# A fused gated long convolution and MLP on one core: the first loads in another order and on two queues, shared copies in tiles of their own, and the last output tile in halves

## The chip, the cores and the metric

The kernel runs on one core of one Trainium2 chip, as one launch. TensorE (PE) multiplies, and PEld is its weight load; VectorE (DVE), ScalarE (ACT) and GpSimd (POOL) do the other arithmetic; SyncE (SP) only issues transfers, and ACT issues some too. The two queues of transfers are q1 (issued by SP) and q10 (issued by ACT) in the profile. The metric is device time in microseconds (us), the median over runs.

## The reference

All inputs are bfloat16, with S = 2048 tokens and D = 512 channels; `F` stands for 1376 hidden columns.

```python
def _A_ref(q, k, v, shift_k, ssm_k, ssm_D):
    k_shift = sum over t in 0..3 of k_pad[:, t:t + S, :] * shift_k[:, 3 - t]
    kv = k_shift * v
    y = irfft(rfft(kv padded to 2S) * rfft(ssm_k padded to 2S))[:S]   # along the tokens
    y = y + kv * ssm_D
    return q * y

x = A_q
h = x + _A_ref(_layernorm(x), A_k, A_v, A_shift_k, A_ssm_k, A_ssm_D)
h2 = h + relu(_layernorm(h) @ w1) @ w2
```

So there is a short convolution over four tokens (the taps), a product with v, a convolution over all tokens with one filter for each channel (ssm_k), a gate with the normalised input, a residual, and an MLP with a residual.

## The kernel before

The order of the work is written out by hand: each engine takes its instructions in the order of the program, and waits by semaphores. PSUM tiles come from a ring of four tiles of two banks each (`bank2`); a fifth tile waits until the users of the first are done with it.

**Opening (L122 to L239).** SP issues, in this order, shift_k (`wsh`, L123), ssm_k (`sk`, 2 MB, L124), and then k and v in four pieces of 512 tokens each, transposed on the way (L134, L136, L137): k0, v0, k1, v1 and so on, about 0.5 MB each. ACT issues two loads of ssm_D (`draw`, 1 KB each, L128). PE runs 22 matmuls on zeros meanwhile (`fill`, L158). POOL makes index tables and two identity matrices (`identw` in float32, then `ident` in bfloat16, L176), `r2` (iota at L180), then `dmask` from ssm_D with 16 small copies (L236), and multiplies `r2` (L238). DVE turns shift_k into float32 (`wf`, L191), works out angles (`_turns`, L44 and L46), then the tables `f1hi` and `f1lo` for stage 1 (L210 to L215), and `tsn` (L222, and `wrap13` at L220). ACT computes the sines (L147) and 16 diagonal matrices `wdiag` (L204), which are the identity scaled by one tap of one group of 128 channels.

**Rows of ssm_k (`to_rows`, L271).** PE transposes ssm_k 128x128 at a time, eight to a PSUM tile, in four steps h = 0 to 3. ACT copies the tiles of h = 0 and 2, DVE that of h = 1, and the tile of h = 3 is copied half by ACT and half by DVE. The same function later turns the product kv around (L388).

**Stage 1 (`stage1`, L286) and taps (`taps`, L329).** The loop at L343 runs gb = 0 to 6. A step of stage 1 is 32 small matmuls into two PSUM tiles; DVE adds `dmask` to half of each (L306), ACT casts the other halves (L309). A tap unit `taps(c, h)` takes a piece c of the tokens and two groups of channels: eight matmuls of `wdiag` with shifted k into one PSUM tile (L333), and one product with v on DVE (L337). Behind step gb stands tap unit (gb // 2, gb % 2), and the last two, (3, 0) and (3, 1), stand ahead of step 6. ACT has sines between its casts (L226, then L262). Behind the loop follow v's rows, step 7, and eight steps for kv, whose tiles ACT and DVE copy into BX (L267, L269).

**Middle and inverse (L402 to L541).** Products in the transformed domain, then `inv1(b, eng)` for b = 0 to 15: twelve matmuls into one PSUM tile, which ACT or DVE copies out as two pieces. At b = 15 both do: ACT groups 0 and 1, DVE groups 2 and 3 of the same tile. The next PE work is `inv2(0)` (tile `pz`, L613).

**MLP (`mlp1`, `mlp2`).** `mlp2(sc)` (L631) runs four tiles of 128 tokens: eleven matmuls of 512 columns (L638), one DVE operation that scales and adds (L641), and a store of 128 KB issued by ACT (L644). The last tile is t = 15.

## Time and profile before

| | us |
|---|---|
| median of 3 runs (215.8 to 216.24) | 216.12 |
| the profiled execution's own time | 215.98 |
| its span, first to last instruction | 214.2 |
| PE busy | 202.7 (95%) |
| DVE busy | 140.8 (66%) |
| ACT busy | 114.9 (54%) |
| POOL busy | 61.6 (29%) |

The span is 1.8 us shorter than the execution's time, which holds what lies ahead of the first and behind the last instruction. The granted PE clock is full in all slices. Busy shares are means over stages. What an edit is worth is read from the stage in which it stands: from what PE waits for there, and from what stands in each queue behind an operation that moves.

### The profile page before, as it was taken

How to read it: one execution, taken by the hardware profiler on the slowest of the kernel's cores; microseconds unless marked ns; L12 is line 12 of the kernel's file. 1: busy time of each engine (PE TensorE's matmuls, PEld its weight loads, DVE VectorE, ACT ScalarE, POOL GpSimd, SP SyncE). 2: the span in 40 equal slices, each digit the busy share in tenths (PEclk: the TensorE clock that was granted, in tenths of full speed). 3: DMA queues.
4: the chain of work that ended last, by engine and by line, in shares of the span. 5: the costliest groups of instructions: out<-in, count | busy, mean ns of one | idle time of the engine just before them, and what ended most of it. 6: DMA issues, size and time to landing. Idle time of an engine off the chain costs nothing. (4 is left out here: it accounts for less than half of the span.)

```text
span 214.2 us, 4311 instructions
## 1 busy us (share of the span) xinstructions
PE 202.7 (95%) x1736; PEld 138.1 (64%) x1736; DVE 140.8 (66%) x243; ACT 114.9 (54%) x185; POOL 61.6 (29%) x116
## 2 busy tenths in 40 slices
PE   7879999999999999999997999999999999999990
PEld 2465555888888888799996964448444844444440
DVE  5968988598778878889753397499249825261121
ACT  6687776687776777645495029601970065027200
POOL 7954704994555500032003012511201120002000
PEclk9999999999999999999999999999999999999999
DMA  5999940001600000036504996977955532410011
GB/s 152 342 226 177 221 77 2 3 5 25 245 0 0 3 0 3 0 98 101 98 3 127 273 216 117 191 129 129 108 58 100 120 74 29 98 55 17 0 51 47
DMA packets 47686, 19.91 MB, mean 93 GB/s; under 512 B 42706, under 2 KB 46132, under 8 KB 47668
## 3 DMA queue, kind: packets, MB, share of 16 engines
q1 hardware_dynamic: 44144, 16.15, 39.2%
q10 hardware_dynamic: 3524, 3.51, 5.7%
q8 instruction: 13, 0.21, 0.4%
q14 instruction: 5, 0.04, 0.1%
HBM read 7.02 MB, written 2.10 MB: 43 GB/s over the span
## 5 line engine op out<-in xcount | busy, mean ns | idle before, releaser
L627 ACT ACTIVATE M<-ps1m 128x512 bf16<-128x512 f32 (+1 forms) x44 | 25.0, 602 | 49.9 <-PE ps1m L625 39.4
L638 PE MATMUL ps2m<-M 128*128 128x512 bf16 (+1 forms) x176 | 38.7, 379 | 0.0
L638 PEld LDWEIGHTS <-M 128*128 128x128 bf16 (+1 forms) x176 | 17.1, 98 | 20.9 <-ACT M L627 0.4
L625 PEld LDWEIGHTS <-w 128*128 128x128 bf16 (+1 forms) x176 | 17.4, 100 | 20.4 <-issue 0.8
L380 POOL TENSOR_TENSOR smc<-st 64x256 fp32r<-64x256 f32 x32 | 22.7, 729 | 11.1 <-PE us L427 10.2
L641 DVE SCALAR_TENSOR_TENSOR M<-ps2m,rstd,M 128x512 bf16<-128x512 f32 x12 | 8.9, 746 | 22.0 <-PE ps2m L638 13.1
L531 PE MATMUL psi<-inv,BK 128*128 128x256 f32 x128 | 23.1, 283 | 0.1
L481 POOL TENSOR_SCALAR rstd<-mv 128x4 f32<-128x4 f32 x8 | 2.2, 275 | 68.9 <-DVE mv L479 68.9
L434 DVE TENSOR_TENSOR BK<-u,ktu 128x512 fp32r<-128x512 f32 x32 | 20.4, 680 | 0.0
L531 PEld LDWEIGHTS psi<-inv,BK 128*128 128x128 f32 x128 | 20.1, 195 | 0.3 <-DVE BK L434 0.3
L625 PE MATMUL ps1m<-xT,w 128*128 128x512 bf16 (+1 forms) x88 | 19.6, 379 | 0.2 <-ACT M L627 0.2
L625 PE MATMUL ps1m<-M,w 128*128 128x512 bf16 (+1 forms) x88 | 19.3, 379 | 0.0
L531 PE MATMUL psi<-inv,BX 128*128 128x256 f32 x64 | 18.2, 286 | 0.0
L407 ACT COPY ktu<-u 128x512 f32<-128x512 f32 x32 | 17.2, 589 | 1.5
L434 DVE TENSOR_TENSOR BX<-us,kts 128x512 fp32r<-128x512 f32 x16 | 11.1, 691 | 8.4 <-PE u L417 6.7
L417 PE MATMUL u<-BK,st 64*128 64x256 f32 x128 | 14.6, 308 | 0.0
L407 ACT COPY kts<-us 128x512 f32<-128x512 f32 x16 | 9.4, 587 | 9.5 <-PE us L427 9.5
L417 PE MATMUL u<-BX,st 64*128 64x256 f32 x128 | 13.0, 284 | 0.0
L309 ACT CAST BK<-ps 128x512 fp32r<-128x512 f32 x16 | 9.4, 585 | 6.5 <-PE ps L294 3.9
L531 PEld LDWEIGHTS psi<-inv,BX 128*128 128x128 f32 x64 | 12.4, 195 | 0.3 <-DVE BK L434 0.2
L477 DVE BATCH_NORM_STATS2 st<-M 128x6 f32<-128x512 bf16 x20 | 12.3, 678 | 0.0
L599 DVE TENSOR_TENSOR qT<-pz,qT 128x2048 bf16<-128x2048 f32 x2 | 4.6, 2291 | 11.3 <-DMA qT<-M 7.3
(123 smaller groups left out, 399.0 us busy)
## 6 DMA issues: line engine op xcount, KB each, us to landing
E<-in_A_ssm_k_dram SPq DMA_DIRECT2D x1, 2048.0 KB
out_dram<-M ACTq DMA_DIRECT2D x16, 128.0 KB
w<-in_B_w_dram SPq DMA_DIRECT2D x1, 1376.0 KB
M<-in_B_w_dram ACTq DMA_DIRECT2D x1, 1280.0 KB
M<-in_A_q_dram SPq DMA_DIRECT2D x8, 128.0 KB
xh<-in_A_q_dram SPq DMA_DIRECT2D x4, 128.0 KB
xr<-in_A_q_dram SPq DMA_DIRECT2D x4, 128.0 KB
M<-in_B_w_dram ACTq DMA_DIRECT2D x1, 96.0 KB
```

Of the source, the lines that this page charges most:

```text
L309: nc.scalar.copy(out=o[1 - rp][:, 1], in_=pv[1 - rp][:, 1])
L380: nc.gpsimd.tensor_tensor(out=smc[pq, c % 4, i, :, 64 * dp:64 * dp + 64], in0=st[pq, ks, 64:128].bitcast(F32), in1=st[pq, ks, 0:64].bitcas ...
L407: nc.scalar.copy(out=kt[:], in_=ps)
L417: nc.tensor.matmul(out=ps[:, dp, 256 * x:256 * x + 256], lhsT=t[pq], rhs=cols((BK, BX)[x], pq, k1, i), start=(i == 0), stop=(i == 1), tile ...
L434: nc.vector.tensor_tensor(out=o, in0=ps[:, :, 256:512].rearrange("p b (g x) -> p b g x", x=8), in1=kt[:].rearrange("p b (g x) -> p b g x", ...
L477: nc.vector.bn_stats(out=st[:, i, :], in_=src[:, i, :])
L531: nc.tensor.matmul(out=o, lhsT=src[:, g // 2, :, g % 2::2].rearrange("p c r -> p (c r)"), rhs=rhs, start=(part == 0), stop=(part == 2), sk ...
L599: nc.vector.tensor_tensor(out=flat(qT[q]), in0=pzs[q][:].rearrange("p i r a n -> p (i r a n)"), in1=flat(qT[q]), op=ALU.mult)
L625: nc.tensor.matmul(out=ps1[:fsz, :].rearrange("p (i t) -> p i t", i=4), lhsT=w1[:, c, fc * P:fc * P + fsz], rhs=hT[sc][:, :, c, :], start= ...
L627: nc.scalar.activation(out=h1T[:fsz, fc, :], in_=ps1[:fsz, :], func=ACT.Relu)
L638: nc.tensor.matmul(out=ps2[:], lhsT=h1T[:ksz, fc, i * P:(i + 1) * P], rhs=w2[:ksz, fc, :], start=(fc == 0), stop=(fc == NFC - 1))
L641: nc.vector.scalar_tensor_tensor(out=o[:], in0=ps2[:], scalar=rstd2[:, t, :], in1=xh[sc][:, i, :], op0=ALU.mult, op1=ALU.add)
```

## The change

- **Loads.** The loads of shift_k and ssm_k move from SP's queue to ACT's, ahead of the two loads of ssm_D. SP's queue then begins with k0. The zeroing of two tiles on DVE comes ahead in the text.
- **Identities.** POOL makes `ident` before `identw`.
- **wdiag.** Of the 16 scalings, the eight for the first two groups of channels go to DVE, the other eight stay on ACT, ahead of the first two sines. `_turns` for t3 and the work on `tsn` change places with the tables f1.
- **Taps.** `taps(0, 0)` and `taps(0, 1)` move ahead of the rows of ssm_k, behind 14 of the matmuls on zeros; six more of these follow them. In the loop, the tap units behind the steps are now (1, 0), (1, 1), (2, 0), none, (2, 1), none.
- **Tiles of their own.** In `to_rows` at h = 3 and in `inv1` at b = 15, ACT's and DVE's parts each get a PSUM tile.
- **Last tile.** For t = 15, `mlp2` runs two halves of 256 columns, each with eleven matmuls, one DVE operation and one store of 64 KB.

In the built program ACT's order at the start is: load of shift_k, load of ssm_k, two loads of ssm_D (the second waits for shift_k's semaphore), a table load, eight scalings, a table load, sines.

```diff
-    nc.sync.dma_start(out=wsh[:], in_=A_shift_k.rearrange("(r p) j -> p r j", p=P))
-    nc.sync.dma_start(out=sk, in_=A_ssm_k.rearrange("(c p) t -> p c t", p=P))
+    nc.scalar.dma_start(out=wsh[:], in_=A_shift_k.rearrange("(r p) j -> p r j", p=P))
+    nc.scalar.dma_start(out=sk, in_=A_ssm_k.rearrange("(c p) t -> p c t", p=P))
     draw = small([DC * P], BF16)
     for dp in range(2):
...
-    fill(bank2("psz")[:, 0, :], 22)
+    psz = bank2("psz")[:, 0, :]
+    fill(psz, 14)
...
-    for t in (identw, ident):
+    for t in (ident, identw):
...
+            if rg < 2:
+                nc.vector.tensor_scalar(out=wdiag[:, rg, j, :], in0=ident[:], scalar1=wf[:, rg, j:j + 1], scalar2=None, op0=ALU.mult)
+            else:
+                nc.scalar.mul(out=wdiag[:, rg, j, :], in_=ident[:], mul=wf[:, rg, j:j + 1])
...
+    taps(0, 0)
+    taps(0, 1)
+    fill(psz, 6)
...
-        pst = bank2("pst").rearrange("p b (i c) -> p (b i) c", i=4)
...
-        for i in range(8):
-            nc.tensor.transpose(out=pst[:, i, :], in_=srcw[:, :, 8 * h + i], identity=identw[:])
...
+        for eng, i0, n in {1: (("D", 0, 8),), 3: (("A", 0, 4), ("D", 4, 4))}.get(h, (("A", 0, 8),)):
+            pst = bank2("pst").rearrange("p b (i c) -> p (b i) c", i=4)[:, 0:n]
+            for i in range(n):
+                nc.tensor.transpose(out=pst[:, i, :], in_=srcw[:, :, 8 * h + i0 + i], identity=identw[:])
...
+    behind = {0: (1, 0), 1: (1, 1), 2: (2, 0), 4: (2, 1)}
...
-        if gb < 6:
-            taps(gb // 2, gb % 2)
+        if gb in behind:
+            taps(*behind[gb])
...
-        ps = bank2("psi").rearrange("p b (i d a n) -> p (b i) d a n", i=2, d=2, a=2)
...
         for e, i0, n in ((eng, 0, 4),) if len(eng) == 1 else ((eng[0], 0, 2), (eng[1], 2, 2)):
+            ps = bank2("psi").rearrange("p b (i d a n) -> p (b i) d a n", i=2, d=2, a=2)[:, 0:n]
...
+            w = D // 2 if t == NT - 1 else D
+            for d0 in range(0, D, w):
+                ps2 = psm.tile([P, D], F32, tag="ps", name="ps2m")[:, 0:w]
```

More of the change, by code (lines that the diff above doesn't have):

```diff
@@ L122 @@
     wsh = consts.tile([P, DC, KS], BF16, name="wsh")
-    nc.sync.dma_start(out=wsh[:], in_=A_shift_k.rearrange("(r p) j -> p r j", p=P))
-    nc.sync.dma_start(out=sk, in_=A_ssm_k.rearrange("(c p) t -> p c t", p=P))
+    zero = consts.tile([P, 512], BF16, name="zero")
+    nc.vector.memset(zero[:], 0.0)
+    nc.vector.memset(kT[0][:, :, 0:16], 0.0)
+    nc.scalar.dma_start(out=wsh[:], in_=A_shift_k.rearrange("(r p) j -> p r j", p=P))
+    nc.scalar.dma_start(out=sk, in_=A_ssm_k.rearrange("(c p) t -> p c t", p=P))
     draw = small([DC * P], BF16)
@@ L128 @@
         nc.scalar.dma_start(out=draw[64 * dp:64 * dp + 1, :], in_=src)
-    zero = consts.tile([P, 512], BF16, name="zero")
-    nc.vector.memset(zero[:], 0.0)
-    nc.vector.memset(kT[0][:, :, 0:16], 0.0)
     for c in range(4):
@@ L194 @@
     _turns(nc, t1[:, 32:64], r1[:], n1c[:], 128, False)
+    f1f = small([64], F32)
+    f1d = small([64], F32)
+    for rg in range(DC):
+        for j in range(KS):
+            if rg < 2:
+                nc.vector.tensor_scalar(out=wdiag[:, rg, j, :], in0=ident[:], scalar1=wf[:, rg, j:j + 1], scalar2=None, op0=ALU.mult)
+            else:
+                nc.scalar.mul(out=wdiag[:, rg, j, :], in_=ident[:], mul=wf[:, rg, j:j + 1])
+    _sin(f1f[:, 0:32], t1[:, 0:32], 128)
+    _sin(f1f[:, 32:64], t1[:, 32:64], 128, neg=True)
     t3 = small([2, 64], I32)
@@ L197 @@
     _turns(nc, t3[:, 1, :], r3[:], n2c[:], 64, False)
-    f1f = small([64], F32)
-    f1d = small([64], F32)
-    _sin(f1f[:, 0:32], t1[:, 0:32], 128)
-    _sin(f1f[:, 32:64], t1[:, 32:64], 128, neg=True)
-    for rg in range(DC):
-        for j in range(KS):
-            nc.scalar.mul(out=wdiag[:, rg, j, :], in_=ident[:], mul=wf[:, rg, j:j + 1])
     dsc = small([2, 64], F32)
@@ L207, with wrap13 @@
     _sin(dsc[:], t3[:], 64)
+    st = stp.tile([P, 32, 192], F32R, name="st")
+    def wrap13(t):
+        nc.vector.tensor_scalar(out=t, in0=t, scalar1=19, scalar2=19, op0=ALU.logical_shift_left, op1=ALU.arith_shift_right)
+    nc.vector.tensor_single_scalar(out=tsn, in_=r2, scalar=n2c[:], op=ALU.mult)
+    wrap13(tsn)
     f1h = small([64], BF16)
@@ L215, with taps @@
             nc.vector.tensor_copy(out=f[rows, :, rg % 2], in_=src[rows, :].rearrange("p (h w v) -> p w v h", h=2, w=2))
-    st = stp.tile([P, 32, 192], F32R, name="st")
-    def wrap13(t):
-        nc.vector.tensor_scalar(out=t, in0=t, scalar1=19, scalar2=19, op0=ALU.logical_shift_left, op1=ALU.arith_shift_right)
-    nc.vector.tensor_single_scalar(out=tsn, in_=r2, scalar=n2c[:], op=ALU.mult)
-    wrap13(tsn)
+    def taps(c, h, each=2):
+        ps = bank2("pkv")
+        for i in range(2):
+            for j in range(KS):
+                nc.tensor.matmul(out=ps[:, i, :], lhsT=wdiag[:, 2 * h + i, j, :],
+                                 rhs=kT[c][:, 2 * h + i, 16 - j:CH + 16 - j], start=(j == 0), stop=(j == KS - 1))
+        for i in range(0, 2, each):
+            vv = vT[:, 2 * h + i:2 * h + i + each, CH * c:CH * c + CH]
+            nc.vector.tensor_tensor(out=vv, in0=ps[:, i:i + each, :], in1=vv, op=ALU.mult)
+    taps(0, 0)
+    taps(0, 1)
+    fill(psz, 6)
     def big_sin(out, turns, scale):
@@ L271, in to_rows @@
     def to_rows(src, h, fl):
-        pst = bank2("pst").rearrange("p b (i c) -> p (b i) c", i=4)
         srcw = src.bitcast(F32).rearrange("p c (a w) -> p (c a) w", w=32)
-        for i in range(8):
-            nc.tensor.transpose(out=pst[:, i, :], in_=srcw[:, :, 8 * h + i], identity=identw[:])
         o = fl.bitcast(I32)
-        for eng, i0, n in {0: (("A", 0, 8),), 1: (("D", 0, 8),), 2: (("A", 0, 8),), 3: (("A", 0, 4), ("D", 4, 4))}[h]:
-            oi, pi = o[:, :, 8 * h + i0:8 * h + i0 + n], pst[:, i0:i0 + n, :]
+        for eng, i0, n in {1: (("D", 0, 8),), 3: (("A", 0, 4), ("D", 4, 4))}.get(h, (("A", 0, 8),)):
+            pst = bank2("pst").rearrange("p b (i c) -> p (b i) c", i=4)[:, 0:n]
+            for i in range(n):
+                nc.tensor.transpose(out=pst[:, i, :], in_=srcw[:, :, 8 * h + i0 + i], identity=identw[:])
+            oi = o[:, :, 8 * h + i0:8 * h + i0 + n]
             if eng == "A":
-                nc.scalar.copy(out=oi.bitcast(F32), in_=pi.rearrange("p i c -> p c i"))
+                nc.scalar.copy(out=oi.bitcast(F32), in_=pst.rearrange("p i c -> p c i"))
             else:
-                nc.vector.tensor_single_scalar(out=oi, in_=pi.bitcast(I32).rearrange("p i c -> p c i"),
+                nc.vector.tensor_single_scalar(out=oi, in_=pst.bitcast(I32).rearrange("p i c -> p c i"),
                                                scalar=0, op=ALU.bitwise_or)
@@ L327, in more_sines @@
             big_sin(st[:, half, 64:128], r2[:, half], 1)
-    def taps(c, h, each=2):
-        ps = bank2("pkv")
-        for i in range(2):
-            for j in range(KS):
-                nc.tensor.matmul(out=ps[:, i, :], lhsT=wdiag[:, 2 * h + i, j, :],
-                                 rhs=kT[c][:, 2 * h + i, 16 - j:CH + 16 - j], start=(j == 0), stop=(j == KS - 1))
-        for i in range(0, 2, each):
-            vv = vT[:, 2 * h + i:2 * h + i + each, CH * c:CH * c + CH]
-            nc.vector.tensor_tensor(out=vv, in0=ps[:, i:i + each, :], in1=vv, op=ALU.mult)
     inv3 = consts.tile([P, 2, 2, 64], F32R, name="inv3")
@@ L522, in inv1 @@
     def inv1(b, eng):
-        ps = bank2("psi").rearrange("p b (i d a n) -> p (b i) d a n", i=2, d=2, a=2)
-        def of(i, parts):
-            g = 4 * b + i
-            o = ps[:, i].rearrange("p d a n -> p (d a n)")
-            for part in parts:
-                src = BX[:, 0] if part == 0 else BK[:, part - 1]
-                rhs = inv3[:].rearrange("p d a n -> p (d a n)") if part == 0 else                     inv12[:, 4 - 2 * part:8 - 2 * part, :].rearrange("p a n -> p (a n)")
-                nc.tensor.matmul(out=o, lhsT=src[:, g // 2, :, g % 2::2].rearrange("p c r -> p (c r)"), rhs=rhs,
-                                 start=(part == 0), stop=(part == 2), skip_group_check=True)
@@ L534, in inv1, with of @@
-        for i, parts in (((0, (0,)), (2, (0,)), (0, (1, 2)), (1, (0, 1, 2)), (2, (1, 2)), (3, (0, 1, 2))) if b == 0 else
-                         [(i, (0, 1, 2)) for i in range(4)]):
-            of(i, parts)
-        for e, i0, n in ((eng, 0, 4),) if len(eng) == 1 else ((eng[0], 0, 2), (eng[1], 2, 2)):
+        for e, i0, n in ((eng, 0, 4),) if len(eng) == 1 else ((eng[0], 0, 2), (eng[1], 2, 2)):
+            ps = bank2("psi").rearrange("p b (i d a n) -> p (b i) d a n", i=2, d=2, a=2)[:, 0:n]
+            def of(i, parts):
+                g = 4 * b + i0 + i
+                o = ps[:, i].rearrange("p d a n -> p (d a n)")
+                for part in parts:
+                    src = BX[:, 0] if part == 0 else BK[:, part - 1]
+                    rhs = inv3[:].rearrange("p d a n -> p (d a n)") if part == 0 else                         inv12[:, 4 - 2 * part:8 - 2 * part, :].rearrange("p a n -> p (a n)")
+                    nc.tensor.matmul(out=o, lhsT=src[:, g // 2, :, g % 2::2].rearrange("p c r -> p (c r)"), rhs=rhs,
+                                     start=(part == 0), stop=(part == 2), skip_group_check=True)
+            for i, parts in (((0, (0,)), (2, (0,)), (0, (1, 2)), (1, (0, 1, 2)), (2, (1, 2)), (3, (0, 1, 2))) if b == 0 else
+                             [(i, (0, 1, 2)) for i in range(n)]):
+                of(i, parts)
@@ L538, in inv1 @@
             for rho in range(2):
                 copy(e, ax[rho][:, :, :, 8 * b + 2 * i0:8 * b + 2 * i0 + 2 * n],
-                     ps[:, i0:i0 + n].rearrange("p i d a n -> p a n (i d)")[:, rho].rearrange("p (n m) c -> p n m c", m=2))
+                     ps.rearrange("p i d a n -> p a n (i d)")[:, rho].rearrange("p (n m) c -> p n m c", m=2))
     lift(0)
@@ L634, in mlp2 @@
             t = 4 * sc + i
-            ps2 = psm.tile([P, D], F32, tag="ps", name="ps2m")
-            for fc in range(NFC):
-                ksz = min(P, DFF - fc * P)
-                nc.tensor.matmul(out=ps2[:], lhsT=h1T[:ksz, fc, i * P:(i + 1) * P], rhs=w2[:ksz, fc, :],
-                                 start=(fc == 0), stop=(fc == NFC - 1))
-            o = ob[t % 3]
-            nc.vector.scalar_tensor_tensor(out=o[:], in0=ps2[:], scalar=rstd2[:, t, :], in1=xh[sc][:, i, :],
-                                           op0=ALU.mult, op1=ALU.add)
-            dst = bass.AP(tensor=out_d.tensor, offset=out_d.offset + t * D, ap=[[16 * D, 4], [64 * D, 32], [1, D]])
-            nc.scalar.dma_start(out=dst, in_=o)
+            o = ob[t % 3]
+            w = D // 2 if t == NT - 1 else D
+            for d0 in range(0, D, w):
+                ps2 = psm.tile([P, D], F32, tag="ps", name="ps2m")[:, 0:w]
+                for fc in range(NFC):
+                    ksz = min(P, DFF - fc * P)
+                    nc.tensor.matmul(out=ps2, lhsT=h1T[:ksz, fc, i * P:(i + 1) * P], rhs=w2[:ksz, fc, d0:d0 + w],
+                                     start=(fc == 0), stop=(fc == NFC - 1))
+                nc.vector.scalar_tensor_tensor(out=o[:, d0:d0 + w], in0=ps2, scalar=rstd2[:, t, :], in1=xh[sc][:, i, d0:d0 + w],
+                                               op0=ALU.mult, op1=ALU.add)
+                dst = bass.AP(tensor=out_d.tensor, offset=out_d.offset + t * D + d0, ap=[[16 * D, 4], [64 * D, 32], [1, w]])
+                nc.scalar.dma_start(out=dst, in_=o[:, d0:d0 + w])
             if hook is not None:
```

## The prediction, made before the changed kernel ran

> **What bounds the kernel now.** I read the page's forty slices first: PE is nine tenths busy or more from the eighth slice almost to the end, at a granted clock of 1.0 throughout, so time is won only where PE stands still, where its work shrinks, or after its last matmul. Then PE's waits (engine, line, what it waited for: total us, times, longest):

> ```profile
> PE ps L294 <- DVE E L283: 1.4, 1, 1.4
> ...
> PE pz L613 <- DVE ax L269: 1.2, 1, 1.2
> PE pst L276 <- DMA E<-in_A_ssm_k_dram: 1.0, 1, 1.0
> ```

> At each of the three stands a part of the change. The opening microseconds, in order of time (start, length, engine, line, operation):

> ```profile
> 1.17 7.36 PE L156 MATMUL psz<-zero 128*128 128x512 bf16 x22 [1.17 <-DVE pbias L143]
> ...
> 1.79 7.35 SPq L134 DMA_TRANSPOSE E<-in_A_k_dram  x1
> ...
> 6.56 5.16 POOL L236 COPY dmask<-E 1x64 bf16<-1x64 bf16 x16
> ...
> 9.19 2.10 SPq L137 DMA_TRANSPOSE E<-in_A_v_dram  x1
> ...
> 9.56 3.84 PE L276 MATMUL pst<-identw,E 128*128 128x128 f32 x32 [1.02 <-DMA E<-in_A_ssm_k_dram]
> ...
> 11.83 1.99 POOL L238 TENSOR_SCALAR G<-G,n2c 128x2048 int32<-128x2048 int32 x1
> ```

> PE fills with zeros until 8.5, then waits for ssm_k (sk below) until 9.56; k's first transpose (k0) sits in the same queue for 7.35 us behind sk, v's (v0) after it. From 14.8 on:

> ```profile
> 14.06 0.69 DVE L283 TENSOR_SCALAR E<-pst 128x512 int32<-128x512 int32 x1 [1.21 <-ACT E L281]
> ...
> 15.81 1.90 PE L333 MATMUL pkv<-E 128*128 128x512 bf16 x8
> ...
> 17.75 1.22 DVE L337 TENSOR_TENSOR E<-pkv,E 128x1024 bf16<-128x1024 f32 x1
> ```

> DVE's half copy waits 1.21 us for ACT's half of the same tile. After it, stage 1 and tap units alternate, one pair per 2.83 us (groups start at 17.65, 20.67, 23.51, 26.34, 29.18), and in windows of 2 us PE is busy for all of it: that stretch is PE's.

> **What the DMA queues do together** decides the opening. Rate first (windows 2.6 to 8.5 and 9.4 to 16 us):

> ```profile
> DMA packets 576, 2.06 MB, mean 349 GB/s; under 512 B 77, under 2 KB 77, under 8 KB 576
> ```
> ```profile
> DMA packets 6054, 1.53 MB, mean 231 GB/s; under 512 B 6054, under 2 KB 6054, under 8 KB 6054
> ```

> sk takes 5.9 us with a slow start (slices then reach 417 to 444 GB/s, so 5.0 without it); a 0.52 MB transpose takes 2.2. Then order: a copy issued on ACT's queue 0.66 us after a transpose on SP's (timeline, then queues from 163.2 to 165.6):

> ```profile
> 162.49 0.55 ACTq L644 DMA_DIRECT2D out_dram<-M  x1
> ```
> ```profile
> 161.83 2.05 SPq L602 DMA_TRANSPOSE M<-M  x1
> ```
> ```profile
> q1 hardware_dynamic: 1949, 0.49, 111.2%
> q10 hardware_dynamic: 5, 0.01, 1.4%
> ```

> ACT's copy (q10) moves next to nothing until SP's transpose (q1) is through. The reverse stands at 117 to 121.5, where q1 isn't listed at all, though a transpose was issued on it at 116.87, after w2 on ACT's queue:

> ```profile
> q10 hardware_dynamic: 1164, 1.19, 87.0%
> ```

> So I take the two queues as served in order of issue.

> **Part 1, loads.** Order now: sk, k0, v0. After: SP issues k0 at about 0.73 at once, ACT issues wsh then sk at about 1.25; SP issues v0 when k0's issue ends (2.0 us by the L137 row, so 2.75). By order of issue: k0, sk, v0. Nothing moved before 2 us then, and little before 3; k0 2.2 us plus some of the slow start, 5.0 to 5.2; sk 5.0 to 5.9 more, 10.0 to 11.1; v0 2.2 more, 12.2 to 13.3. I take 10.7 and 13.0. Before, v0 lands near 9.4 + 4.4 = 13.8, so moving sk saves about 0.8 of loading, the part of the start in which nothing flowed.

> [...]

> [...]

> **Part 2, wdiag, table, ssm_D.** Eight scalings go to DVE: the trace has none; ACT's L204 took 4.76/16 = 0.30, DVE's 64-wide L46 0.18, so 1.5 to 2.4 us for eight, beginning after wf at 2.95. ACT, now with a scaling ahead of its first sine, has a second table load in its built order (1.28 by the L147 row): wf 2.95 + 1.28 + 2.4 + 1.28 + 0.64 for sines = 8.6; DVE's ten f1 operations (2.1, L210 to L215) then end at 10.7. All of it lies under v0's landing at 13.0; if wsh should wait behind k0, 2 us later, it still does, barely.

> ssm_D's two loads now stand behind sk in ACT's queue: about 10.8 instead of in time for POOL at 6.56. Behind them on POOL: 16 dmask copies (5.16, but the median of one is 0.234 and the longest 1.33, beside DVE's L222 and L220, which now run earlier: 16 medians would be 3.7, so 3.0 to 3.7) and L238, 1.99, which wrap13(r2) on DVE waits for: 10.8 + 3.4 + 0.2 + 2.0 = 16.4. DVE gets there at 17.2. Hidden by 0.8; with 5.16 copies late by 1.0.

> **Part 3, two tap units ahead of sk's rows.** They leave PE's bound stretch: 2 x 1.83 (15.81 to 17.65) = 3.66. But their DVE products stand ahead of DVE's row copies and need v0: from 13.0, 1.22 + 1.22 + 1.23 + 0.69, less 0.09 overlap at three joints (as 20.78 + 1.22 against the next start at 21.92), = 4.1 to 4.2. Stage 1 starts at 17.2 instead of 14.81. Against the 3.66 that is a gain of 1.3.

> Two steps lose the tap unit behind them. Over gb 3, gb 4 and the unit after: PE 1.0 + 1.0 + 1.83 = 3.8, ACT (four casts at 0.58, a sine of 1.06, one of 1.24) 4.6. With four PSUM tiles PE can't run further ahead: cost 0 to 0.8, taken 0.8, as both cover each other no longer. DVE's half copy without its 1.2 wait is already in the 4.2. In v's rows the same edit frees up to 0.4, but DVE's eight 1.18 us BX copies follow at once (9.46 us, busy without a gap), so I count 0. Opening: -1.3 + 0.8 = -0.5; bounds -1.3 (v0 at 12.2) to +0.9 (v0 at 14.4). Fills 22 to 20: under the waits, 0. The ident order: POOL's two forms swap, 0.

> **Part 4, inverse step b = 15.**

> ```profile
> 115.77 0.37 ACT L267 CAST BX<-psi 128x256 fp32r<-128x256 f32 x1 [1.26 <-PE psi L531]
> ...
> 116.45 0.42 DVE L269 CAST BX<-psi 128x256 fp32r<-128x256 f32 x1 [0.83 <-ACT ax L267]
> ```
> ```profile
> 117.35 0.35 PE L613 MATMUL pz<-core,BX 128*128 128x256 f32 x1 [1.17 <-DVE ax L269]
> ```

> With own tiles ACT starts six matmuls of 0.12 sooner and DVE at 115.8, when PE is done: pz 0.65 earlier, bounds 0 to the 1.17 of PE's wait. PE is fully busy behind it, so it carries: -0.65.

> **Part 5, last tile in halves.**

> ```profile
> 209.04 0.75 DVE L641 SCALAR_TENSOR_TENSOR M<-ps2m,rstd,M 128x512 bf16<-128x512 f32 x1 [1.63 <-PE ps2m L638]
> ```

> PE: 22 matmuls of 256 columns; L613 runs such, with a weight load each, 0.114 apart: 2.5 against 11 x 0.217 = 2.4, +0.1. DVE's half: between 0.42 (L269 at 256) and 0.75, taken 0.45: -0.3. The store: 128 packets of 1 KB at 24.7% of 16 engines (166.2 to 169.2), 47 ns each, four engines, 32 in a row = 1.5; the 256 B packets above cost 22 ns, so 512 B some 30: -0.5, bounds 0 to -0.8. Sum -0.7 (-1.0 to +0.1).

> **Sum.** Profiled execution 215.98 (span 214.2 and 1.8 around it): -0.5 - 0.65 - 0.7 = -1.85. The median of the runs is 216.12, 0.14 above: 214.3.

> **Rivals.** (a) Mixing is slow, the slower side: one transpose beside ACT's copies was issued in 6.39 us (147.55) instead of 1.93. If k0 and v0 take 6.4 each from 0.7 and land 2.2 later, v0 comes at 15.7: opening +2.2, 217.0. It decides from v0 at 15.2, where the sum passes 216.5. For: that row; against: 117 to 121.5, where the copy kept its rate. Chance 0.22. (b) The bytes bound it: v0 at 13.8 as before, opening +0.3, 215.1: 0.16, still faster. (c) POOL's copies stay 5.16 in all and sk lands at 11.5, v0 at 13.7: stage 1 at 17.9 (opening +0.2), and wrap13(r2) waits for POOL to 19.0, 1.1 more: 216.1, 0.12. The forecast: 0.50.

> **Numbers.** What a measurement tells from no change is about 0.2%, 0.43 us. Faster 0.50 + 0.16 = 0.66, same 0.12, slower 0.22. Eight in ten: 213.3 (v0 at 12.2, full store gain) to 216.6.

> **What would show it.** Stage 1's first matmul near 17.2, released by DVE; k0's issue 2 us long, v0's stretched until sk is nearly in; the first tap product ended by v's DMA at 13.0; POOL's dmask waiting for ssm_D; pz waiting about 0.5; from the last DVE operation to the span's end under 4.0 instead of 4.4. Wrong if sk lands before k0 (the order of issue isn't kept), or if v0 comes after 14.

## The result and the profile after

The changed kernel takes 219.98 us (median of four runs, 219.35 to 220.19) where the kernel before takes 216.12: a ratio of 1.0171, with a 95% interval of 1.0144 to 1.0197. It is 3.9 us slower; the prediction said 1.8 faster. The profiled execution of it took 219.35, with a span of 217.3, so 3.1 us more span than the 214.2 before; it is 0.6 under the median, so the places below, which are read from its trace, account for 3.1 of the 3.9. Line numbers below are those of each kernel; the changed one is some 10 lines longer (taps L233, product with v L237, rows L296 and L301, stage 1 L312, pz L622, gate L608).

PE's waits in the changed kernel (engine, line, what it waited for: total us, times, longest):

```profile
PE pkv L233 <- DMA E<-in_A_k_dram: 4.8, 1, 4.8
...
PE ps L312 <- DVE E L301: 0.9, 1, 0.9
PE pz L622 <- DVE ax L287: 0.7, 1, 0.7
...
PE ps1m L634 <- DVE xT L609: 0.4, 1, 0.4
```

Two of the three waits of before are smaller, as meant: ahead of stage 1 (1.4 to 0.9) and ahead of pz (1.2 to 0.7). The third, for ssm_k, is gone, but in its place stands a wait of 4.8 for k0, and at the head of the MLP there is a new one of 0.4. The chain that ended last, for its first 24 us (start, length, what):

```profile
0.72 10.09 DMA E<-in_A_k_dram
10.81 0.04 issue
10.85 5.30 PE pkv L233 x16
16.16 1.29 PE psz L156 x6
17.45 3.60 PE pst L296 x32
...
21.08 0.70 DVE E L301
...
21.91 1.07 PE ps L312 x32
```

k0, first in SP's queue, lands at 10.81. PE then does the 16 tap matmuls in 5.30 us, six matmuls on zeros, and only then the rows of ssm_k, which had been in since 10.24 by its queue's completions. Stage 1 starts at 21.91 instead of 14.81. Why k0 is so late stands in the two queues from 5 to 9 us:

```profile
q10 hardware_dynamic: 360, 1.47, 91.3%
q1 hardware_dynamic: 361, 0.09, 10.3%
```

The columns are packets, MB and share of the 16 engines' time. Both queues moved the same number of packets, 360 and 361; but one of ACT's carries 4 KB of ssm_k, one of SP's some 250 B of k0. The granted clock (us, busy time and matmuls of PE, then PEclk) tells why the taps took 5.30 instead of twice 1.83:

```profile
8.00:11.00 3.00, 0.15 (x1) 1.00 1.20 304
...
12.00:14.00 2.00, 2.00 (x6) 0.50 1.01 193
...
15.00:16.00 1.00, 1.00 (x7) 1.00 1.18 222
```

PE stood still from 6.06 to 10.85 and was at half its clock within 0.7 us of its restart; the tap matmuls followed each other by 0.427 us there instead of 0.216. POOL's dmask, which the prediction followed too, came as forecast (copies 3.04 us, behind a wait for ssm_D):

```profile
10.42 3.04 POOL L254 COPY dmask<-E 1x64 bf16<-1x64 bf16 x16 [4.03 <-DMA E<-in_A_ssm_D_dram]
```

The rest of the kernel, from PE's and VectorE's rows:

```profile
120.77 0.36 PE L622 MATMUL pz<-core,BX 128*128 128x256 f32 x1 [0.71 <-DVE ax L287]
```
```profile
125.11 2.29 DVE L608 TENSOR_TENSOR qT<-pz,qT 128x2048 bf16<-128x2048 f32 x1 [4.49 <-PE pz L622]
...
212.90 0.48 DVE L652 SCALAR_TENSOR_TENSOR M<-ps2m,rstd,M 128x256 bf16<-128x256 f32 x1 [0.72 <-PE ps2m L650]
```

How far each place stands behind its time in the kernel before, which locates the loss and the gains:

| place | before | after | behind by |
|---|---|---|---|
| stage 1, first matmul | 14.81 | 21.91 | 7.10 |
| v's rows, first transpose | 36.98 | 41.09 | 4.11 |
| middle, first matmul | 51.63 | 55.64 | 4.01 |
| pz, first matmul | 117.35 | 120.77 | 3.42 |
| MLP, first matmul | 124.89 | 128.72 | 3.83 |
| last VectorE operation, end | 209.79 | 213.38 | 3.59 |
| span, end | 214.2 | 217.3 | 3.1 |

The loss arises ahead of stage 1, but for 0.4 at the head of the MLP. The two tap units that left the loop pay back 3.0, pz gains 0.6, the last tile gains 0.2 and the store 0.5.

### The profile page after: what moved, and what is told of

Read it like the earlier page. It is cut to its first block, busy times and chain, and to the rows that moved or that the text cites. A ratio compares the mean times of both kernels' runs of the same rounds, so it can differ in the third digit from the quotient of the medians.

```text
span 217.3 us, 4328 instructions
## 1 busy us (share of the span) xinstructions
PE 202.5 (93%) x1736; PEld 139.5 (64%) x1745; DVE 142.2 (65%) x252; ACT 113.3 (52%) x178; POOL 59.3 (27%) x116
## 4 chain that ended last, share of the span: by engine, by line
PE 82%; DVE 5%; DMA 5%; ACT 4%; issue 2%; DVEq 0%
PE ps2m L650 17%; PE ps1m L634 14%; PE psi L541 11%; PE u L426 9%; PE us L436 9%; PE pkv L233 7%; PE ps L312 7%; PE pz L622 5%; DMA E<-in_A_k_dram 5%; PE pst L296 3%; ACT BX L280 2%; DVE st L486 1%; ACT M L636 1%; DVE qT L608 1%; DVE BK L324 1%
## 5 line engine op out<-in xcount | busy, mean ns | idle before, releaser
L650 PE MATMUL ps2m<-M 128*128 128x512 bf16 (+3 forms) x183 | 38.6, 366 | 0.2
L650 PEld LDWEIGHTS <-M 128*128 128x128 bf16 (+1 forms) x187 | 18.2, 98 | 20.1 <-ACT M L636 0.4
L634 PEld LDWEIGHTS <-w 128*128 128x128 bf16 (+1 forms) x176 | 17.3, 100 | 20.9 <-issue 0.8
L652 DVE SCALAR_TENSOR_TENSOR M<-ps2m,rstd,M 128x512 bf16<-128x512 f32 (+1 forms) x13 | 9.1, 706 | 22.9 <-PE ps2m L650 13.7
L416 ACT COPY ktu<-u 128x512 f32<-128x512 f32 x32 | 17.2, 589 | 1.5
L443 DVE TENSOR_TENSOR BX<-us,kts 128x512 fp32r<-128x512 f32 x16 | 11.1, 692 | 8.4 <-PE u L426 6.7
L233 PEld LDWEIGHTS <-E 128*128 128x128 bf16 x64 | 6.3, 104 | 13.3 <-DVE E L224 4.8
L233 PE MATMUL pkv<-E 128*128 128x512 bf16 x31 | 9.1, 445 | 4.8 <-DMA E<-in_A_k_dram 4.8
L237 DVE TENSOR_TENSOR E<-pkv,E 128x1024 bf16<-128x1024 f32 (+1 forms) x9 | 9.8, 1104 | 4.8 <-PE pkv L233 4.7
```

The lines of the kernel that those rows point to most:

```text
L233: nc.tensor.matmul(out=ps[:, i, :], lhsT=wdiag[:, 2 * h + i, j, :], rhs=kT[c][:, 2 * h + i, 16 - j:CH + 16 - j], start=(j == 0), stop=(j = ...
L416: nc.scalar.copy(out=kt[:], in_=ps)
L443: nc.vector.tensor_tensor(out=o, in0=ps[:, :, 256:512].rearrange("p b (g x) -> p b g x", x=8), in1=kt[:].rearrange("p b (g x) -> p b g x", ...
L634: nc.tensor.matmul(out=ps1[:fsz, :].rearrange("p (i t) -> p i t", i=4), lhsT=w1[:, c, fc * P:fc * P + fsz], rhs=hT[sc][:, :, c, :], start= ...
L650: nc.tensor.matmul(out=ps2, lhsT=h1T[:ksz, fc, i * P:(i + 1) * P], rhs=w2[:ksz, fc, d0:d0 + w], start=(fc == 0), stop=(fc == NFC - 1))
```

## The experiments

The theory after the result: the two queues take turns packet by packet (the 360 and 361 above), so ssm_k's large packets starve k0, and PE's fixed order turns the late k0 into a late everything, with the clock's fall on top. Rivals: the first transposed load is slow by itself; the diagonals on VectorE, the second table load or the steps without a tap unit cost the time. "Before" in the verdicts is the kernel before on the same chip, 215.96 to 216.03 us.

**ssm_k behind k0 on one queue.**

```diff
-    nc.scalar.dma_start(out=sk, in_=A_ssm_k.rearrange("(c p) t -> p c t", p=P))
...
             nc.sync.dma_start_transpose(out=kT[c][:, :, 16:CH + 16], in_=k_d[0:CH, :])
+            nc.sync.dma_start(out=sk, in_=A_ssm_k.rearrange("(c p) t -> p c t", p=P))
```

> The changed kernel, but ssm_k is issued on SP's queue, between k0 and v0; shift_k and ssm_D stay on ACT's. If the loss comes from two queues that share the DMA engines packet by packet, k0 now has them to itself: k0 lands near 5 to 6 us instead of 10.81, sk near 10.5, v0 near 13; PE's wait for k0 (4.8 us) is gone, the first taps start near 7.2 (after the diagonals on DVE, which end at 7.14), stage 1 near 17.2 instead of 21.91, and the kernel takes 214.5 to 215.5 us. If the transposed piece is slow by itself at the start, or the steps that lost a tap unit are what costs, k0 still lands near 10 or stage 1 moves and the time doesn't: 218 us or more.

Measured: 215.64 us (214.69 to 216.13), ratio to before 0.9962 (0.9935 to 0.9989). PE's rows:

```profile
7.08 3.62 PE L233 MATMUL pkv<-E 128*128 128x512 bf16 x16
...
15.68 2.07 PE L296 MATMUL pst<-identw,E 128*128 128x128 f32 x16 [1.23 <-DVE E L237]
...
18.63 0.23 PE L312 MATMUL ps<-f_hi,E 64*128 64x128 bf16 x2 [0.88 <-DVE E L301]
```

k0 is in at 5.11, the taps run at 7.08 at full clock in 3.62, stage 1 starts 3.3 earlier than in the changed kernel, and 4.3 us of the loss are gone (the 0.4 at the head of the MLP among them): the rivals that leave k0 slow or blame the diagonals, the tables or the steps without a tap unit fall, since all of these are unchanged here. One thing more differs: ssm_D no longer waits behind ssm_k, and POOL's copies begin at 6.54 instead of 10.42. In the changed kernel POOL was through with them and with the multiplication behind them at 15.53, six us ahead of stage 1, so this isn't what the run won back. The time lies just above what was expected, because ssm_k came at 12.29 and v0 at 14.31, not near 10.5 and 13: VectorE's products with v0, which free the PSUM tiles, hold PE's rows up for 1.23, and stage 1 starts at 18.63 instead of 17.2.

**ssm_k in 1 KB packets**, to test the taking of turns by itself.

```diff
-    nc.scalar.dma_start(out=sk, in_=A_ssm_k.rearrange("(c p) t -> p c t", p=P))
+    for i in range(4):
+        nc.scalar.dma_start(out=sk[:, :, 512 * i:512 * i + 512],
+                            in_=A_ssm_k[:, 512 * i:512 * i + 512].rearrange("(c p) t -> p c t", p=P))
```

> The changed kernel, but ssm_k's load on ACT's queue is cut into four along the tokens, so that its packets have 1 KB instead of 4 KB. If the DMA engines take one packet of each queue in turn, k0's 250 B packets now come up four times as often per byte of ssm_k: k0 lands near 7.5 us (7.0 to 8.5) instead of 10.81, PE waits under 2 us for it, its clock stays full, stage 1 starts near 17.3 to 18.5 and the kernel takes 215.3 to 217 us. If the engines share by bytes, or k0 is held up by anything else than the size of ssm_k's packets, k0 still lands between 10 and 11 and the time stays at 219 to 220.

Measured: 224.18 us (222.77 to 226.01), ratio 1.0379 (1.0328 to 1.0429). k0 came as expected, the time did not. The queues from 4.2 to 5.2 us, then ACT's rows:

```profile
q10 hardware_dynamic: 280, 0.29, 81.4%
q1 hardware_dynamic: 281, 0.07, 31.6%
```
```profile
7.54 6.80 ACTq L133 DMA_DIRECT2D E<-in_A_ssm_D_dram  x2
14.44 1.28 ACT L205 ACT_TABLE_LOAD   x1 [14.44 <-DMA E<-in_A_v_dram]
```

Again one packet for one packet, 280 and 281 in 1 us instead of 360 in 4, and k0 is in at 7.53, where 7.5 was expected. So in both stretches the two queues shared by packets, not by bytes and not by order of issue. The time was lost elsewhere: with three more loads the two of ssm_D wait in ACT's queue for the semaphores of k0 and v0 (landed at 7.53 and 14.09), and ACT's eight diagonals stand behind them, so PE waits 6.7 us for a diagonal:

```profile
16.19 3.59 PE L235 MATMUL pkv<-E 128*128 128x512 bf16 x8 [6.74 <-ACT E L205]
```

**k0 first with no tap moved**, the price of the order of loads alone, on top of the run with own tiles and halves below.

```diff
-    nc.sync.dma_start(out=sk, in_=A_ssm_k.rearrange("(c p) t -> p c t", p=P))
...
             nc.sync.dma_start_transpose(out=kT[c][:, :, 16:CH + 16], in_=k_d[0:CH, :])
+        nc.sync.dma_start(out=sk, in_=A_ssm_k.rearrange("(c p) t -> p c t", p=P))
...
-    fill(bank2("psz")[:, 0, :], 22)
+    fill(bank2("psz")[:, 0, :], 38)
```

> The run with tiles of their own and halves (214.14 us), where SP issues k0 ahead of ssm_k, with no tap unit moved and 38 matmuls on zeros instead of 22 so that PE's clock stays full. It prices the order of the loads alone. By the run with ssm_k behind k0 on one queue, ssm_k lands near 12.3 instead of 9.3, stage 1 starts near 17.2 instead of 14.35, and the kernel takes 216.7 to 217.3 us; the two tap units ahead of the rows (215.64) then won back some 1.4 of it. By the prediction's terms (ssm_k in at 10.7) stage 1 starts near 15.7 and the kernel takes 215.3 to 215.7 us.

Measured: 216.65 us (216.5 to 217.06), ratio 1.0021 (0.9997 to 1.0044), so 2.5 above its base of 214.14 and just under the first range expected. PE's rows:

```profile
12.26 3.99 PE L278 MATMUL pst<-identw,E 128*128 128x128 f32 x32
17.13 0.23 PE L294 MATMUL ps<-f_hi,E 64*128 64x128 bf16 x2 [0.88 <-DVE E L283]
```

k0 was in at 5.56 and ssm_k at 11.53, against 9.28 in the base: the delay of 2.25 is about what k0 takes by itself. The rows started at 12.26, when the 38 matmuls on zeros were done, 0.7 after ssm_k; stage 1 at 17.13. So the order of the loads makes some 1.8 of the 2.5, and the 38 matmuls, 16 too many to end before ssm_k was in, the other 0.7. The run with ssm_k behind k0 (215.64), which has the two tap units ahead of the rows and the rest of the change, wins back 1.0, not all of it.

**A warm PE.** 34 matmuls on zeros ahead of the taps.

```diff
-    fill(psz, 14)
+    fill(psz, 34)
```

> The changed kernel with 34 matmuls on zeros ahead of the first taps instead of 14, so that PE has no idle stretch before k0 lands at 10.8. If the lower granted clock after the idle 4.8 us makes the 16 tap matmuls take 5.30 us, they now take 3.7, stage 1 starts 1.4 to 1.6 us earlier and the kernel takes 217.7 to 218.2 us. If the tap matmuls are slow for another reason (operands written by DMA meanwhile, diagonals late), the time stays at 219.4 to 220.

Measured: 217.91 us (217.39 to 218.31), as expected. The clock in the same window as above:

```profile
12.00:14.00 2.00, 2.00 (x11) 1.00 1.07 189
```

Eleven matmuls in the 2 us where the changed kernel did six. Stage 1 starts at 20.24, 1.67 earlier: this is the share of the clock, with k0 exactly as late as before (10.82). Useless matmuls on PE were worth 1.65 us between the profiled executions (219.35 and 217.7) and 2.07 between the medians.

**Taps behind the rows again**, with the loads of the changed kernel.

```diff
-    fill(psz, 14)
+    fill(psz, 22)
...
-    taps(0, 0)
-    taps(0, 1)
-    fill(psz, 6)
...
-    behind = {0: (1, 0), 1: (1, 1), 2: (2, 0), 4: (2, 1)}
+    behind = {i: (i // 2, i % 2) for i in range(6)}
```

> The changed kernel with its loads, but taps (0,0) and (0,1) go back into the loop behind the rows of ssm_k, and the 22 matmuls on zeros stand together again. If PE's order (rows of ssm_k queued behind taps that wait for k0) makes the loss, and the loads alone cost only what sk lands later (10.24 instead of 9.43), the rows start near 10.3 instead of 17.29, stage 1 near 15.5, and the kernel takes 215.5 to 216.5 us. If the loads themselves, the diagonals on DVE or the second table load make the loss, it stays above 218.

Measured: 216.8 us (216.35 to 218.01), ratio 1.0034 (1.0008 to 1.006), 0.3 above the range. PE's order, with the clock's fall that it brings, therefore makes 3.2 of the loss (219.98 to 216.8). What stays is 2.7 more than the run with the same tiles and halves but the loads of before (214.14, below): ssm_k is in 1.0 later (10.31 against 9.28) and the head of the MLP has its 0.4. In the profiled execution (217.32) the clock, which the expectation left out, makes another 1.4: PE stood 2.74 us ahead of the rows, and they took 5.44 us instead of 4.06:

```profile
10.45 5.44 PE L293 MATMUL pst<-identw,E 128*128 128x128 f32 x32 [2.74 <-DMA E<-in_A_ssm_k_dram]
```
```profile
12.00:14.00 2.00, 2.00 (x11) 0.50 1.07 206
```

The median doesn't rest on this fall of the clock: over the profiled execution the mean granted clock was 0.992, but in six of the ten it was 0.995 to 1.0, and these took 216.35 to 216.96, still 2.2 to 2.8 above 214.14. With 1.0 for ssm_k and 0.4 for the MLP, about 1 us of that stays unexplained, since none of the six was traced.

**Own tiles and halves alone**, on the kernel before; then each by itself. The diff is the one shown of the change for `to_rows` and `inv1` (own tiles) and for `mlp2` (halves), and nothing else.

> The kernel before with only the tiles of their own (rows of ssm_k at h = 3, inverse step b = 15) and the last output tile in halves. If these parts work by themselves as in the trace of the changed kernel (pz 0.65 earlier with 0.4 of it lost again ahead of the MLP, 0.7 at the end), it takes 214.9 to 215.3 us; if the 0.4 isn't lost here, 214.5 to 214.8, with up to 0.3 more from the rows at h = 3. If the wait of pz only moves on to the next tile, 216 us.

Measured: 214.14 us (214.03 to 214.35), ratio 0.9895 (0.9862 to 0.9928): 1.85 faster than before, better than expected. PE's rows:

```profile
14.35 0.23 PE L294 MATMUL ps<-f_hi,E 64*128 64x128 bf16 x2 [0.88 <-DVE E L283]
```
```profile
116.11 0.36 PE L613 MATMUL pz<-core,BX 128*128 128x256 f32 x1 [0.71 <-DVE ax L269]
```

Stage 1 starts 0.46 earlier than before (14.81), of which ssm_k's arrival makes 0.15; pz starts 1.24 earlier (117.35). The MLP keeps it here: its first matmul comes at 123.71, 1.18 earlier, and the 0.4 isn't lost.

> The kernel before with only the tiles of their own. The trace of the run with both parts shows stage 1 starting 0.46 us earlier (of which 0.14 by ssm_k) and pz 1.24 earlier than before, and the MLP keeping it: 214.8 to 215.1 us, two thirds of what both parts gain. If the last tile makes most of the gain, it stays at 215.5 or above.

Measured: 214.97 us (214.85 to 216.26, and one run of eleven at 290.83), ratio 0.9938 (0.9914 to 0.9962): 0.99 faster, as expected.

> The kernel before with only the last output tile in halves. From the last operation on VectorE to the span's end it takes 3.9 instead of 4.4 us and the last operation ends 0.2 earlier: 215.2 to 215.5 us. If two stores on four DMA engines each take as long as one, 215.8 to 216.1.

Measured: 215.23 us (215.1 to 216.73), ratio 0.9969 (0.9952 to 0.9987): 0.73 faster, as expected. 0.99 + 0.73 = 1.72 of the 1.85.

**One more instruction.**

```diff
     nc.vector.memset(pbias[:], 0.5 * TURN)
+    nc.vector.memset(pbias[:], 0.5 * TURN)
```

> The changed kernel with one more tiny operation on VectorE at the start (pbias is set twice, 0.06 us). The gate on pz (L608) began 0.42 us after its last wait ended in the changed kernel and in the two runs with ssm_k on ACT's queue, 0.04 after it in the two with ssm_k on SP's; VectorE's queue is one semaphore instruction longer in the first three. If the gap belongs to the place in the queue, it is gone or elsewhere here, PE's wait for xT (0.4) is gone, and the time is 0.3 to 0.4 under the changed kernel's. If it belongs to the transfers that run then, the gap and the wait stay.

Measured: 219.06 us (218.38 to 219.59), 0.9 under the changed kernel; with four runs each that scatter over 1 us, the time says less than the trace. VectorE's row of the gate:

```profile
124.53 2.29 DVE L609 TENSOR_TENSOR qT<-pz,qT 128x2048 bf16<-128x2048 f32 x1 [4.15 <-PE pz L623]
```

It starts 4.00 after pz's first matmul (120.53) instead of 4.34, and PE's wait for xT is gone. A gap of 0.43 now stands one instruction earlier, between the two semaphore instructions ahead of the gate, where VectorE waits for pz anyway. So the gap goes with the place in VectorE's queue, the 192nd of the trace's records, in both kernels, and not with the operation. In the run with ssm_k behind k0, whose queue is one record shorter, the 192nd record shows no gap (0.03), so the count alone doesn't settle it; what happens at that place isn't shown.

**Three tries for a better version**, all on the run of 214.14 us. First one tap unit in PE's 0.9 us between rows and stage 1:

```diff
     for h in range(4):
         to_rows(sk, h, kfl)
+    taps(0, 0)
...
-        if gb < 6:
-            taps(gb // 2, gb % 2)
+        if gb < 5:
+            taps((gb + 1) // 2, (gb + 1) % 2)
```

> The run with tiles of their own and halves (loads and queues as in the kernel before), and tap unit (0,0) between the rows of ssm_k and stage 1, the others one step earlier, so that step 5 has none. If PE's 0.9 us ahead of stage 1 is free for a tap unit and a step without one costs 0.35, it gains 0.5: 213.5 to 213.9 us. If the product with v0 (landing 13.9) on DVE delays the first step, or the step without a tap unit costs 0.9, it is 214.1 to 214.8.

Measured: 214.78 us (214.65 to 216.26), the second form expected. PE's row names the wait that took the gain:

```profile
19.59 0.21 PE L294 MATMUL ps<-f_hi,E 64*128 64x128 bf16 x1 [1.37 <-ACT BK L309]
```

VectorE adds to step 0 only at 18.24 instead of 15.95, behind the product with v0, wrap13(r2) and six small operations. The next two move these:

```diff
-    wrap13(r2)
...
         stage1(kfl, BK, gb, dmask)
+        if gb == 1:
+            wrap13(r2)
```

The six small operations on pi4, k1o, rof, esc and ebi go behind step 0 in the same way.

> The run with one tap unit behind the rows (214.78 us), with the six small operations on pi4, k1o, rof, esc and ebi moved behind stage 1's step 0 on VectorE and wrap13(r2) behind step 1. There PE waited 1.4 us for step 0's tiles, since VectorE's product with v0 and these operations stood ahead of step 0's additions (18.24 instead of 15.95 us). If that wait is what ate the gain, it is gone and the kernel takes 213.3 to 213.8 us. If VectorE has no room for them later, 214.3 us or more.

> The run with tiles of their own and halves (214.14 us), with the same operations moved and no tap unit moved. PE's 0.5 us wait for ACT's first casts, which wait for VectorE's first addition at 15.95, should go: 213.6 to 213.8 us. If VectorE has no room for them later, 214.1 or more. Beside the run with the tap unit moved too it shows what the tap unit alone is worth.

Measured: 214.64 us (214.44 to 216.11) with the tap unit and 215.38 us (215.26 to 215.86) without. Neither gains: PE's wait for ACT's casts is 1.5 in all in both (0.5 in the run of 214.14, 1.8 with the tap unit alone), now at step 2, since wrap13(r2) takes 1.8 to 2.0 us there (1.22 at its old place) and the additions of step 2 start behind it. wrap13(r2) has no room there; what stood between the rows and stage 1 stood well. The tap unit by itself is worth 0.74 (215.38 to 214.64), but only where VectorE is the limit already. The fastest version seen stays the one with only own tiles and halves, 214.14.

## Why the prediction was wrong, point by point

- **What bounds the kernel.** The three waits were the right places, and two of the three edits there did what was said. (The forty slices hold one 7 behind the eighth, the twenty-second, which holds the wait of pz.)
- **The step that failed: "So I take the two queues as served in order of issue".** From it came k0 at 5.0 to 5.2; it landed at 10.81, behind ssm_k at 10.24. The tell named in the prediction (ssm_k before k0) happened. The two pairs of rows it rested on show something else, how late the later transfer starts. In the one, ACT's store moved its first packet at 165.45, 2.96 after its issue began, where a store issued with no transposing transfer under way (183.73) began 1.18 after its issue. In the other, the issue of the transposing transfer lasted 5.99 us, and its first packet came at 121.52. Once both queues had packets to move, as in the changed kernel from 3.5 to 9 us, they moved them at the same pace, 467 and 465. Why the later transfer starts so late in those two places isn't shown.
- **No term for PE's own queue.** The sum followed v0, and v0 came at 13.02, as forecast (13.0), though by luck: the order of the loads ahead of it was another. But the moved taps stand ahead of the rows in PE's order, so the load that decides is k0. Stage 1 came at 21.91 instead of 17.2. From the trace, against the 14.81 of before: the first matmuls on zeros end 2.5 earlier; the wait for a load is 3.8 longer (4.8 instead of 1.0); the taps add 5.3, of which 1.6 is the lower clock (5.30 less 3.66; the run with a warm PE gave back 1.67); the six matmuls on zeros, which no longer hide, add 1.3; the rows and the wait behind them take 0.8 less. That is the 7.1.
- **The loads' sizes.** With k0 first on one queue it does land at 5.11, as said. But ssm_k then comes at 12.29 (11.53 in the run with k0 first and no tap moved) instead of 10.7, and v0 at 14.31 instead of 13.0: ssm_k took 5.97 us behind k0 in the second of these, as against the 5.9 of before, so its slow start is paid there too. From v0 on, the chain of VectorE's products and copies was right: 14.31 + 4.3 = 18.63, where 4.1 to 4.2 was forecast. So even in the order forecast, the opening would not have gained 0.5: that run is 1.5 slower than own tiles and halves alone.
- **Steps without a tap unit.** From stage 1 to v's rows took 22.17 before and 19.18 after: 2.99 less, so 3.66 less 0.67, where 0.8 was taken. Right.
- **wdiag, table, ssm_D.** Hidden, as forecast: VectorE's eight scalings took 1.51, the second table load came at 7.10, the copies of dmask took 3.04. The tables f1 ended at 12.09 instead of 10.7, since the work on `tsn` stands ahead of them, which cost nothing.
- **Inverse step b = 15.** 0.65 forecast; between the middle and pz the changed kernel gains 0.59. 0.41 was lost again at the gate, by the gap described above, which no row of before could show. At h = 3 the own tile is worth about 0.3 more, which the prediction had folded into its chain.
- **Last tile.** 0.7 forecast, 0.73 measured alone; VectorE's half took 0.48 (0.45 was taken).
- **Rivals.** Rival (a) had the right place, two mixed queues, and the wrong victim: it let v0 be late and priced nothing for k0. Slower had a chance of 0.22; none of its forms reached 219.98.

## What to carry to other kernels

## What the runs showed of the hardware that was not expected

- **PE's clock at the start and after idle stretches.** The page shows the clock as full from the start, but in the kernel before the matmuls on zeros follow each other by 0.43 us until 6.15, where the trace's first clock record stands, and by 0.22 after it:

```profile
4.00:6.00 2.00, 2.00 (x6) 1.00 0.97 399
6.00:8.00 2.00, 2.00 (x11) 1.00 1.02 420
```

In the changed kernel that record stands at 4.62, and the matmuls on zeros change from 0.43 to 0.22 there too; its granted clock was then 1.00 until 11.45, 0.50 until 14.86 (3.41 us) and 1.00 again until 216.25. After idle stretches of 0.84 us (own tiles and halves), 1.02 (the kernel before) and 1.68 (tap unit and block moved) PE did the rows at full clock, in 4.06, 3.84 and 4.07 us. After 2.02 us (own tiles only), 2.74 (taps behind the rows) and 4.79 (the changed kernel) the granted clock was 0.50 for about 3.4 us, from 0.6 to 1.3 us behind PE's restart, and that cost 1.4 to 1.6 us each. After 6.74 us (1 KB packets) eight tap matmuls took 3.59 us, where the eight ahead of them had taken 1.89. Whether the length of the idle stretch alone decides, or also where it lies, isn't shown. The 2.02 is the profiled execution of own tiles only, 216.26 us against a median of 214.97: there the same 22 matmuls on zeros ended at 7.4 instead of 8.5. On one chip the kernel before took 217.4 to 217.7 in 5 of its 29 repeats, with a mean granted clock of 0.992, and 215.8 to 216.1 in the others (0.992 to 1.0); none of the five was traced, so their cause isn't shown.

- **Two loads in ACT's queue held ACT's arithmetic.** In the run with 1 KB packets two 1 KB loads, waiting for the semaphores of k0 and v0, were issued from ACT's queue only between 7.54 and 14.34, and ACT's first operation came at 14.44 instead of the 3.34 of the changed kernel.
- **Transposed loads behind other loads were long in their issue.** v0's lasted 8.38 us in the changed kernel, until 10.53, just after ssm_k was in (10.24), and 9.11 with ssm_k ahead of it on the same queue, until 12.06, just before (12.29). In the kernel before, k0's took 7.35 behind ssm_k and v0's 2.10.
